# Two expert units as one from the denominator's absolute value on, and weights converted in larger steps

## The chip, the cores and the metric

The kernel runs on one core of a Trainium2 chip. A core has five engines that work through their own queues in order: PE (matmul), DVE (vector), ACT (scalar, with activation functions), POOL (elementwise work) and SP (here it only issues DMAs). The metric is the device time in microseconds (us); the time of several runs is given by its median. A profiled execution is one more run, of which a trace is kept.

## The reference

A delta-rule attention gives the rows of x, and a feed-forward layer with a rational activation follows. The shapes: 4 batches, 8 heads, 768 steps, head size 48; 3072 tokens, width 384, hidden width 2048.

```
for t in range(S):                                # S = 768, per batch and head
    y[t] = q[t] @ state
    v_old = state.T @ k_n[t]                      # k_n: keys, normalized
    state = state + beta[t] * outer(k_n[t], v[t] - v_old)
x = y, heads side by side                         # 3072 x 384
h = x @ w_in                                      # 3072 x 2048
P = a0 + a1*h + a2*h^2 + a3*h^3
Q = 1 + |b0|*|h| + |b1|*h^2
out = (P / (Q + 1e-6)) @ w_out                    # 3072 x 384
```

The two weight matrices come as 64-bit floats, the rest as 32-bit floats.

## The kernel before

The time axis is cut into 12 chunks of 64 steps (`NCH`). Within a chunk the attention is done in blocks by matmuls; 256 tokens (4 batches of 64, `TG`) leave each chunk. The hidden width is cut into 8 units of 256 columns (`NU`), so the feed-forward work is 96 units, numbered through: unit n is chunk n // 8, columns n % 8. Numbers are kept as sums of two 16-bit floats (`split16`), so a product takes three matmul passes (`PASSES`).

The weights are read once, ahead of the units. `load_in(i)` and `load_out(i)` take one unit each; `to_f32` turns 64-bit words into 32-bit floats, in pieces of 256 columns (`w_in`) and 192 columns (`w_out`): a DMA into a staging tile, an absolute value on ACT (L316), a clamp on POOL (L317), and three DVE instructions (L318, and L325 twice). The staging tiles take turns among the nine buffers of the tags mw, mu and mr (three each, `MB`). A unit's weights are scaled by a power of two found from their sums of squares, and split into two 16-bit parts; of `w_out` one half of each unit is scaled and subtracted on POOL (L243, L230), the other on DVE (L232). `tables` and `scalars` make the six coefficients per unit (`tab`, and `msc` for a chunk).

A unit's steps: `hidden(n)` makes the product ph in PSUM (18 matmuls, L808). `numerator(n)` takes its absolute value and a linear term on ACT (L826, L828), then three DVE instructions (L830, L832, L833), with an absolute value of the denominator on ACT between (L831). `quotient(n)` takes the logarithm and the exponential of minus that on ACT (L841, L842), which is the reciprocal, then three DVE instructions (L844, L845, L846; a correction of the quotient, whose middle result goes into the next unit's ph in PSUM), and a product on POOL (L847). `accumulate(n)` multiplies both 16-bit parts g by the weights (12 matmuls, L862).

One loop over n writes the program: numerator of unit n, quotient of n-1, one eighth of the attention of later chunks (`attention`), accumulate of n-2, hidden of n+1. The DVE instructions of units keep this order among themselves (`in_order`); all others are put in each engine's queue by a scheduler, from priorities and its own model of durations. ph has two PSUM buffers, each of u, w and r three SBUF buffers. The attention for the last chunks runs out before the units do, so the last units stand alone.

## Time and profile before

| | |
|---|---|
| time, median of 3 runs | 843.07 us (842.95 to 843.18) |
| profiled execution: its own time, its span | 849.25 us, 845.5 us |
| mean granted PE clock | 0.944 |
| PE, DVE, ACT, POOL busy | 74%, 88%, 73%, 40% of the span |
| DMA moved | 111.46 MB, mean 132 GB/s |

The span runs from the first to the last instruction. In a row of the profile, L844 is line 844 of the kernel, "mg<-mu,msc,mr" are the tiles written and read, "128x512" is partitions by elements, and x96 is how often; behind the bar stand the busy time in all, the mean duration in ns, and how long the engine had been idle before such instructions and for whom. All 111 MB are issued from the queues of SP and ACT.

### The profile page before, as it was taken

The page shows a single profiled execution, that of the slowest core. Times are in us where ns is not written, and L with a number is a line of the kernel's source. Part 1 is how long each engine was busy: PE and PEld are TensorE (multiplying, and loading weights), DVE is VectorE, ACT ScalarE, POOL GpSimd, SP SyncE. Part 2 cuts the span into 40 slices and gives each one's busy share as a digit, 9 for nine tenths or more (in the row PEclk, how much of TensorE's full clock was granted, in tenths as well). Part 3 has the DMA queues.
Part 4 walks back from the last instruction along what each step waited for, and adds up shares of the span by engine and source line. Part 5 has one row for each costly group of instructions (what it writes and reads, how often), then busy time and mean ns, then how long its engine had stood idle before and what let it go on. Part 6 is the DMA issues. An engine that isn't in the chain of part 4 may idle for free.

```text
span 845.5 us, 23179 instructions
## 1 busy us (share of the span) xinstructions
PE 627.7 (74%) x9264; PEld 493.8 (58%) x9264; DVE 740.2 (88%) x1405; ACT 617.1 (73%) x1278; POOL 338.1 (40%) x322
## 2 busy tenths in 40 slices
...
GB/s 237 249 212 170 225 155 170 123 140 169 157 130 165 146 120 191 146 140 183 93 145 187 71 176 150 119 193 105 98 167 111 110 103 80 76 2 21 1 19 19
DMA packets 466507, 111.46 MB, mean 132 GB/s; under 512 B 431328, under 2 KB 463072, under 8 KB 466400
## 3 DMA queue, kind: packets, MB, share of 16 engines
...
## 4 chain that ended last, share of the span: by engine, by line
DVE 34%; PE 19%; DMA 17%; SPq 11%; ACT 10%; issue 7%; POOL 1%; ACTq 0%; DVEq 0%; POOLq 0%
PE ph L808 7%; PE po L862 5%; DVE ph L845 4%; DVE w_out L325 4%; DVE mg L844 3%; DVE mw L830 3%; DVE mu L833 3%; DVE mu L832 3%; SPq L119 3%; PE pu L401 2%; DMA tq<-xdq 2%; DMA gd<-g 2%; DMA tk<-xdk 2%; SPq L475 2%; DVE mu L846 2%
## 5 line engine op out<-in xcount | busy, mean ns | idle before, releaser
L862 PE MATMUL po<-w_out,mg 128*128 128x384 f16 x1152 | 226.5, 339 | 33.3 <-DVE mg L844 20.9
L847 POOL TENSOR_TENSOR mg<-mu,mr 128x512 f16<-128x512 f32 x96 | 124.8, 1300 | 258.1 <-DVE mu L846 203.8
L808 PE MATMUL ph<-xT,w_in 128*128 128x256 f16 x1728 | 216.3, 280 | 14.1 <-DVE mu L846 11.2
L808 PEld LDWEIGHTS <-w_in 128*128 128x128 f16 x1728 | 169.8, 101 | 51.1 <-DVE mu L846 14.4
L862 PEld LDWEIGHTS <-mg 128*128 128x128 f16 x1152 | 109.5, 101 | 103.4 <-DVE mg L844 27.7
L401 PEld LDWEIGHTS <-kbd 128*128 128x128 f16 x1680 | 66.7, 109 | 47.8 <-issue 43.3
L830 DVE SCALAR_TENSOR_TENSOR mw<-mr,msc,ph 128x512 f32<-128x512 f32 x96 | 71.1, 741 | 22.1 <-ACT mu L828 21.9
L831 ACT ACTIVATE mw<-mw 128x512 f32<-128x512 f32 x96 | 60.4, 629 | 39.7 <-DVE mw L830 39.2
L845 DVE SCALAR_TENSOR_TENSOR ph<-mw,msc,mg 128x512 f32<-128x512 f32 x96 | 81.4, 848 | 1.0
L844 DVE SCALAR_TENSOR_TENSOR mg<-mu,msc,mr 128x512 f16<-128x512 f32 x96 | 81.1, 844 | 0.0
L826 ACT ACTIVATE mr<-ph,msc 128x512 f32<-128x512 f32 x96 | 65.2, 679 | 18.7 <-PE ph L808 6.9
L828 ACT ACTIVATE mu<-ph,coef,msc 128x512 f32<-128x512 f32 x96 | 74.2, 773 | 0.0
L846 DVE SCALAR_TENSOR_TENSOR mu<-mu,msc,ph 128x512 f32<-128x512 f32 x96 | 71.1, 741 | 1.4
L833 DVE SCALAR_TENSOR_TENSOR mu<-mu,msc,ph 128x512 f32<-128x512 f32 x96 | 70.7, 736 | 1.0
L841 ACT ACTIVATE mr<-mw,msc 128x512 f32<-128x512 f32 x96 | 69.2, 721 | 1.7
L401 PE MATMUL pu<-z,ebd 128*128 128x48 f16 x1728 | 54.9, 185 | 18.1 <-DVE z L232 13.5
L401 PEld LDWEIGHTS <-ebd 128*128 128x128 f16 x1728 | 53.9, 98 | 21.7 <-issue 19.4
L832 DVE TENSOR_TENSOR mu<-ph,mu 128x512 f32<-128x512 f32 x96 | 65.5, 682 | 0.0
L842 ACT ACTIVATE mr<-mr 128x512 f32<-128x512 f32 x96 | 60.3, 628 | 1.3
L401 PEld LDWEIGHTS <-wbd 128*128 128x128 f16 x1152 | 37.7, 99 | 35.9 <-issue 34.8
L230 POOL TENSOR_TENSOR mm<-m,mm 128x1024 f16<-128x1024 f32 x12 | 29.2, 2436 | 73.6 <-ACT mm L226 64.5
L401 PE MATMUL pm<-tq,kbd 128*128 128x64 f16 x576 | 27.0, 220 | 20.1 <-DMA tq<-xdq 18.3
...
## 6 DMA issues: line engine op xcount, KB each, us to landing
...
```

What stands on the lines that cost most here:

```text
L401: nc.tensor.matmul(dst[p][:, h], head(bd, lp, p * H + h), head(rt, rp, p * H + h), start=start and n == 0 and h == 0, stop=stop and n == l ...
L808: nc.tensor.matmul(ph[:, i], w_in[:, f2, wp, cc, i * P : (i + 1) * P], x[:, xp, cc], start=k == 0, stop=k == 3 * NCC - 1,)
L828: nc.scalar.activation(u, ph, AF.Identity, scale=A3, bias=a2)
L830: in_order(nc.vector.scalar_tensor_tensor(out=w, in0=z, scalar=B0, in1=ph, op0=ALU.add, op1=ALU.mult))
L832: in_order(nc.vector.tensor_mul(u, ph, u))
L833: in_order(nc.vector.scalar_tensor_tensor(out=u, in0=u, scalar=A1, in1=ph, op0=ALU.add, op1=ALU.mult))
L841: nc.scalar.activation(r, w, AF.Ln, bias=Q0)
L844: in_order(nc.vector.scalar_tensor_tensor(out=g[:, 0], in0=u, scalar=A0, in1=r, op0=ALU.add, op1=ALU.mult))
L845: in_order(nc.vector.scalar_tensor_tensor(out=t, in0=w, scalar=Q0, in1=g[:, 0], op0=ALU.add, op1=ALU.mult))
L846: in_order(nc.vector.scalar_tensor_tensor(out=u, in0=u, scalar=A0, in1=t, op0=ALU.add, op1=ALU.subtract))
L847: nc.gpsimd.tensor_mul(g[:, 1], u, r)
L862: nc.tensor.matmul(po[p], g[:, gp, i, p * P : (p + 1) * P], w_out[:, f2, wp, i], start=f2 == lo and i == 0 and k == 0, stop=f2 == hi - 1 a ...
```

## The change

Two neighbouring units, an even and an odd one, become one from the absolute value of the denominator on. `numerator` still works by units of 512 elements up to L821; at the odd unit the absolute value, logarithm and exponential follow at once, over 1024 elements (L824, L825, L826). `quotient(m)` works on pair m: three DVE instructions of 1024 elements (L837, L838, L839) and one POOL product (L840). The correction's middle result goes into w in SBUF instead of the next unit's ph. u, w and z of a pair are one tile mx with two buffers; g of a pair is one tile mg with two buffers. In the loop the quotient of pair n/2 - 1 is written at even n, behind the even unit's numerator, and accumulate comes three units later instead of two.

The weights are handled in four steps of two units (`NS`): one scale for 512 columns, words in groups of 768 per unit (two DMAs of 768 KB a step), staged in the two mx buffers; the absolute value and the clamp work in place. Both halves of `w_out` are split on ACT and DVE. `dynamic_dma_scratch_size=2048` is set where the program is built; the rest follows from the counts (`GRP = 2` steps are the same four units as before).

```diff
-    MB = 3
+    MB = 2
...
+    NS = NU // 2
...
-    def to_f32(t, src, nm, keep=MIN_NORMAL):
+    def to_f32(t, srcs, nm, keep=MIN_NORMAL):
         n = t.shape[-1]
-        st = staged([P, n, 2], U32, "ws" + nm)
-        nc.sync.dma_start(out=st.rearrange("p f w -> p (f w)"), in_=src)
-        wl, wh = st[..., 0], st[..., 1]
-        a = sb.tile([P, n], F32, tag="mg", name="wa" + nm, bufs=MB)
-        nc.scalar.activation(a, wh.bitcast(F32), AF.Abs)
-        nc.gpsimd.tensor_scalar(a, a, 3.0e38, keep, op0=ALU.min, op1=ALU.max)
-        nc.vector.tensor_scalar(
-            t, a.bitcast(U32), 3, KEEP, op0=ALU.logical_shift_left, op1=ALU.bitwise_and
-        )
...
+        st = sb.tile([P, len(srcs), n, 2], U32, tag="mx", name="ws" + nm, bufs=MB)
+        for h, src in enumerate(srcs):
+            w, x = st[:, h], t[:, h]
+            nc.sync.dma_start(out=w.rearrange("p (a f) w -> p a (f w)", a=src.shape[1]), in_=src)
+            wl, wh = w[..., 0], w[..., 1]
+            nc.scalar.activation(x.bitcast(F32), wh.bitcast(F32), AF.Abs)
+            nc.gpsimd.tensor_scalar(x.bitcast(F32), x.bitcast(F32), 3.0e38, keep, op0=ALU.min, op1=ALU.max)
+            nc.vector.tensor_scalar(x, x, 3, KEEP, op0=ALU.logical_shift_left, op1=ALU.bitwise_and)
+            for word, scalar, op0 in ((wh, 0xC0000000, ALU.bitwise_and), (wl, 29, ALU.logical_shift_right)):
+                nc.vector.scalar_tensor_tensor(out=x, in0=word, scalar=scalar, in1=x, op0=op0, op1=ALU.bitwise_or)
...
-        for j in range(2):
-            if j == 0:
-                split16((w_out[:, i, 0, j], w_out[:, i, 1, j]), to[j].bitcast(F32), ss[:, 1:2])
-            else:
-                scaled(to[j].bitcast(F32), ss[:, 1:2])
-                split16((w_out[:, i, 0, j], w_out[:, i, 1, j]), to[j].bitcast(F32), eng=nc.gpsimd)
+        for i in us:
+            split16((w_out[:, i, 0], w_out[:, i, 1]), t[:, i % 2], ss[:, 1:2])
...
     def numerator(n):
...
+        if i == 0:
+            both[m] = {"x": sb.tile([P, 3, 2, 2, TG], F32, tag="mx", name=f"mx{m}", bufs=MB)}
+        u, w, z = (both[m]["x"][:, x, i] for x in range(3))
         nc.scalar.activation(z, ph, AF.Abs, scale=B1)
         nc.scalar.activation(u, ph, AF.Identity, scale=A3, bias=a2)
         in_order(nc.vector.scalar_tensor_tensor(out=w, in0=z, scalar=B0, in1=ph, op0=ALU.add, op1=ALU.mult))
-        nc.scalar.activation(w, w, AF.Abs)
         in_order(nc.vector.tensor_mul(u, ph, u))
         in_order(nc.vector.scalar_tensor_tensor(out=u, in0=u, scalar=A1, in1=ph, op0=ALU.add, op1=ALU.mult))
+        if i == 1:
+            w, r = (both[m]["x"][:, x].rearrange("p i a t -> p (i a t)") for x in (1, 2))
+            nc.scalar.activation(w, w, AF.Abs)
+            nc.scalar.activation(r, w, AF.Ln, bias=Q0)
+            nc.scalar.activation(r, r, AF.Exp, scale=-1.0)
...
-    def quotient(n):
+    def quotient(m):
...
-        t = unit[min(n + 1, NCH * NU - 1)]["ph"]
-        nc.scalar.activation(r, w, AF.Ln, bias=Q0)
-        nc.scalar.activation(r, r, AF.Exp, scale=-1.0)
-        g = sb.tile([P, 2, 2, TG], F16, tag="mg", name=f"mg{n}", bufs=MB)
...
+        x = d.pop("x").rearrange("p x i a t -> p x (i a t)")
+        u, w, r = (x[:, i] for i in range(3))
+        g = d["g"] = sb.tile([P, 2, 2, 2, TG], F16, tag="mg", name=f"mg{m}", bufs=2)
+        g0, g1 = (g[:, i].rearrange("p i a t -> p (i a t)") for i in range(2))
+        in_order(nc.vector.scalar_tensor_tensor(out=g0, in0=u, scalar=A0, in1=r, op0=ALU.add, op1=ALU.mult))
+        in_order(nc.vector.scalar_tensor_tensor(out=w, in0=w, scalar=Q0, in1=g0, op0=ALU.add, op1=ALU.mult))
+        in_order(nc.vector.scalar_tensor_tensor(out=u, in0=u, scalar=A0, in1=w, op0=ALU.add, op1=ALU.subtract))
+        nc.gpsimd.tensor_mul(g1, u, r)
...
-    for n in range(N + 2):
+    for n in range(N + 3):
...
-        if 0 <= n - 1 < N:
-            quotient(n - 1)
+        if n % 2 == 0 and 2 <= n <= N:
+            quotient(n // 2 - 1)
         attention(*divmod(n + SHIFT, NU))
-        if 0 <= n - 2 < N:
-            accumulate(n - 2)
+        if 0 <= n - 3 < N:
+            accumulate(n - 3)
...
+    nc = _bacc.Bacc("TRN2", target_bir_lowering=False, num_devices=1, dynamic_dma_scratch_size=2048)
```

The change moves instructions. Three places show it. In the rows, ph_88 is the product of unit 88, mr88, mu88 and mw88 are its three tiles before, and mx43 and mg43 are the tiles of pair 43 (units 86 and 87) after. The first place is ACT's queue near the end, at units 88 to 90, before:

```order
L826 ACTIVATE mr89_13763<-ph_89_13744,msc_11_13589 128x512
L828 ACTIVATE mu89_13765<-ph_89_13744,coef_99,msc_11_13589 128x512
L842 ACTIVATE mr88_13716<-mr88_13716 128x512
L831 ACTIVATE mw89_13767<-mw89_13767 128x512
L841 ACTIVATE mr89_13763<-mw89_13767,msc_11_13589 128x512
L842 ACTIVATE mr89_13763<-mr89_13763 128x512
L826 ACTIVATE mr90_13815<-ph_90_13796,msc_11_13589 128x512
L828 ACTIVATE mu90_13817<-ph_90_13796,coef_99,msc_11_13589 128x512
```

and ACT's queue at units 86 to 88, after:

```order
L817 ACTIVATE mx43_12604<-ph_87_12627,msc_10_11890 128x512
L818 ACTIVATE mx43_12604<-ph_87_12627,coef_99,msc_10_11890 128x512
L748 ACTIVATE sf_11_12490<-sf_11_12490,kp_11_0_12549 128x1
L748 ACTIVATE sf_11_12490<-sf_11_12490 128x2
L824 ACTIVATE mx43_12604<-mx43_12604 128x1024
L825 ACTIVATE mx43_12604<-mx43_12604,msc_10_11890 128x1024
L817 ACTIVATE mx44_12685<-ph_88_12666,msc_11_12571 128x512
L818 ACTIVATE mx44_12685<-ph_88_12666,coef_99,msc_11_12571 128x512
L826 ACTIVATE mx43_12604<-mx43_12604 128x1024
```

What stood between a denominator and the next unit's first two instructions (L826, L828) is now L824 and L825 of double length, and L817 and L818 of the even unit stand behind them.

The second place is DVE's queue at the same units; before:

```order
L830 SCALAR_TENSOR_TENSOR mw88_13720<-mr88_13716,msc_11_13589,ph_88_13697 128x512
L832 TENSOR_TENSOR mu88_13718<-ph_88_13697,mu88_13718 128x512
L833 SCALAR_TENSOR_TENSOR mu88_13718<-mu88_13718,msc_11_13589,ph_88_13697 128x512
L844 SCALAR_TENSOR_TENSOR mg87_13727<-mu87_13671,msc_10_12856,mr87_13669 128x512
L845 SCALAR_TENSOR_TENSOR ph_88_13697<-mw87_13673,msc_10_12856,mg87_13727 128x512
L846 SCALAR_TENSOR_TENSOR mu87_13671<-mu87_13671,msc_10_12856,ph_88_13697 128x512
L830 SCALAR_TENSOR_TENSOR mw89_13767<-mr89_13763,msc_11_13589,ph_89_13744 128x512
L832 TENSOR_TENSOR mu89_13765<-ph_89_13744,mu89_13765 128x512
L833 SCALAR_TENSOR_TENSOR mu89_13765<-mu89_13765,msc_11_13589,ph_89_13744 128x512
```

and after:

```order
L819 SCALAR_TENSOR_TENSOR mx43_12604<-mx43_12604,msc_10_11890,ph_87_12627 128x512
L820 TENSOR_TENSOR mx43_12604<-ph_87_12627,mx43_12604 128x512
L821 SCALAR_TENSOR_TENSOR mx43_12604<-mx43_12604,msc_10_11890,ph_87_12627 128x512
L819 SCALAR_TENSOR_TENSOR mx44_12685<-mx44_12685,msc_11_12571,ph_88_12666 128x512
L820 TENSOR_TENSOR mx44_12685<-ph_88_12666,mx44_12685 128x512
L821 SCALAR_TENSOR_TENSOR mx44_12685<-mx44_12685,msc_11_12571,ph_88_12666 128x512
L837 SCALAR_TENSOR_TENSOR mg43_12691<-mx43_12604,msc_10_11890 128x1024
L838 SCALAR_TENSOR_TENSOR mx43_12604<-mx43_12604,msc_10_11890,mg43_12691 128x1024
L839 SCALAR_TENSOR_TENSOR mx43_12604<-mx43_12604,msc_10_11890 128x1024
L819 SCALAR_TENSOR_TENSOR mx44_12685<-mx44_12685,msc_11_12571,ph_89_12708 128x512
L820 TENSOR_TENSOR mx44_12685<-ph_89_12708,mx44_12685 128x512
L821 SCALAR_TENSOR_TENSOR mx44_12685<-mx44_12685,msc_11_12571,ph_89_12708 128x512
```

The quotient's three instructions stood behind each unit's numerator; now they stand behind the even unit's only, and the odd unit's numerator (ph_87) is followed at once by that of the next even unit (ph_88).

The third place is ACT's queue in the middle, at unit 63 and the next chunk's first. The names g, gl, kp, sh and z are attention tiles and scalars. Before:

```order
L228 ACTIVATE z_9_2_11304<-pu_9_10922,zmask_85 128x768
L516 ACTIVATE g_11_11123<-pg_11_11074 128x1024
L831 ACTIVATE mw63_11010<-mw63_11010 128x512
L761 ACTIVATE kp_8_0_10846<-kp_8_0_10846 128x1
L226 CAST gl_11_11127<-g_11_11123 128x768
L841 ACTIVATE mr63_11006<-mw63_11010,msc_7_9757 128x512
L777 ACTIVATE kp_8_0_10846<-kp_8_0_10846 128x1
L842 ACTIVATE mr63_11006<-mr63_11006 128x512
```

and after:

```order
L824 ACTIVATE mx31_10044<-mx31_10044 128x1024
L503 ACTIVATE g_11_10248<-pg_11_10199 128x1024
L825 ACTIVATE mx31_10044<-mx31_10044,msc_7_8947 128x1024
L228 ACTIVATE sh_10_10846<-S16_133,sc_10_9303 128x768
L226 CAST gl_11_10252<-g_11_10248 128x768
L826 ACTIVATE mx31_10044<-mx31_10044 128x1024
L817 ACTIVATE mx32_10286<-ph_64_10267,msc_8_10006 128x512
L818 ACTIVATE mx32_10286<-ph_64_10267,coef_99,msc_8_10006 128x512
```

The copy of g and the cast to gl now stand between the odd unit's denominator and the next even unit's two instructions, which come behind the exponential.

127 lines of the change are left out of this document (56 added, 71 removed).

## The prediction

> **What bounds the kernel now.** I read the engine table of the page first, then the busy time by stretches of the run, then the groups with their shapes kept apart, and last the timeline near the end, where the moved work stands alone. The page says that no engine is full over the whole span:
>
> ```profile
> PE 627.7 (74%) x9264; PEld 493.8 (58%) x9264; DVE 740.2 (88%) x1405; ACT 617.1 (73%) x1278; POOL 338.1 (40%) x322
> ```
>
> The stretches tell more (columns: stretch, its length, busy us of each engine, granted clock, DMA share, GB/s). I cut where the weights begin and end, where the first unit starts, and where the DVE's attention work has nearly run out:
>
> ```profile
> core 0: us, PE busy (x) PEld busy (x) DVE busy (x) ACT busy (x) POOL busy (x), PEclk, DMA share, GB/s
> 18.00:134.00 116.00, 35.64 (x582) 30.57 (x581) 111.32 (x311) 81.15 (x215) 66.32 (x90) 0.99 0.93 206
> 134.00:150.00 16.00, 11.96 (x141) 9.28 (x142) 7.51 (x27) 11.84 (x36) 6.99 (x6) 0.63 0.93 159
> 150.00:704.00 554.00, 454.22 (x7111) 360.80 (x7111) 486.58 (x863) 409.49 (x818) 214.14 (x171) 0.93 0.82 139
> 704.00:845.00 141.00, 124.85 (x1424) 92.28 (x1421) 126.09 (x197) 108.07 (x200) 37.67 (x29) 0.99 0.14 28
> ```
>
> While the weights are converted (18 to 134 us) DVE is busy 111.3 of 116 us, and the DMA engines 93%. In the main loop DVE leads with 88%, PE has 82%. At the end DVE has 89%, with no DMA to speak of. So DVE's instructions are the right thing to count, but 67 us of DVE idleness in the loop say that its order and its waits count as well. The changed groups:
>
> ```profile
> L845 DVE SCALAR_TENSOR_TENSOR ph<-mw,msc,mg 128x512 f32<-128x512 f32 x96 | 81.4, 848 | 1.0
> L844 DVE SCALAR_TENSOR_TENSOR mg<-mu,msc,mr 128x512 f16<-128x512 f32 x96 | 81.1, 844 | 0.0
> L846 DVE SCALAR_TENSOR_TENSOR mu<-mu,msc,ph 128x512 f32<-128x512 f32 x96 | 71.1, 741 | 1.4
> L232 DVE SCALAR_TENSOR_TENSOR z<-pu,zmask,z 128x768 f16<-128x768 f32 x36 | 36.3, 1007 | 2.5 <-ACT z L228 2.3
> L847 POOL TENSOR_TENSOR mg<-mu,mr 128x512 f16<-128x512 f32 x96 | 124.8, 1300 | 258.1 <-DVE mu L846 203.8 <-ACT ob L876 12.9 <-ACT kp L761 9.4
> L240 ACT ACTIVATE sq<-q 128x768 f32<-128x768 f32 x12 | 10.1, 842 | 20.6 <-DMA q<-in_q_dram 11.3 <-DMA k<-in_k_dram 5.6 <-DVE nrm L492 2.8
> ```
>
> **Term 1, fewer and longer DVE instructions.** The same kind of instruction takes 741 ns for 512 elements (L846) and 1007 for 768 (L232): 1.04 ns per element and 209 ns fixed. One of 1024 takes 741 + 512 x 1.04 = 1273 ns. L844 and L845 cost more than L846 at equal length, and the view of one line says why: the median is that of L846, a few are far longer.
>
> ```profile
> L844 DVE SCALAR_TENSOR_TENSOR mg<-mu,msc,mr x96: 731/746/1898, 159.8 to 834.9; 128x512 f16<-128x512 f32 x96
> ```
>
> The excess of the mean is 844 - 746 = 98 ns. L844 reads both tensors from SBUF; L846, which reads one from PSUM, has no such excess. After the change all three read two SBUF tensors, so I give each 0.1 us more. A pair of units costs 2 x (844 + 848 + 741) = 4866 ns before and 3 x (1273 + 100) = 4119 after: 0.75 us less. For the 36 pairs up to unit 71, which lie in the loop under attention work, that is 27 us of DVE time.
>
> [...]
>
> [...]
>
> **Term 2, the new wait at the odd unit.** The end of the run shows the unit's bare rhythm, DVE first, then ACT, then PE:
>
> ```profile
> 822.02 0.74 DVE L830 SCALAR_TENSOR_TENSOR mw<-mr,msc,ph 128x512 f32<-128x512 f32 x1
> 822.68 0.68 DVE L832 TENSOR_TENSOR mu<-ph,mu 128x512 f32<-128x512 f32 x1
> 823.40 0.75 DVE L833 SCALAR_TENSOR_TENSOR mu<-mu,msc,ph 128x512 f32<-128x512 f32 x1
> 824.07 0.74 DVE L844 SCALAR_TENSOR_TENSOR mg<-mu,msc,mr 128x512 f16<-128x512 f32 x1
> 824.85 0.76 DVE L845 SCALAR_TENSOR_TENSOR ph<-mw,msc,mg 128x512 f32<-128x512 f32 x1
> 825.64 0.75 DVE L846 SCALAR_TENSOR_TENSOR mu<-mu,msc,ph 128x512 f32<-128x512 f32 x1
> 826.31 0.74 DVE L830 SCALAR_TENSOR_TENSOR mw<-mr,msc,ph 128x512 f32<-128x512 f32 x1
> ```
>
> ```profile
> 822.80 0.63 ACT L831 ACTIVATE mw<-mw 128x512 f32<-128x512 f32 x1 [0.99 <-DVE mw L830]
> 823.46 0.72 ACT L841 ACTIVATE mr<-mw,msc 128x512 f32<-128x512 f32 x1
> 824.22 0.63 ACT L842 ACTIVATE mr<-mr 128x512 f32<-128x512 f32 x1
> 824.75 0.67 ACT L826 ACTIVATE mr<-ph,msc 128x512 f32<-128x512 f32 x1
> 825.32 0.77 ACT L828 ACTIVATE mu<-ph,coef,msc 128x512 f32<-128x512 f32 x1
> ```
>
> ```profile
> 822.16 2.14 PE L808 MATMUL ph<-xT,w_in 128*128 128x256 f16 x18
> 824.14 2.20 PE L862 MATMUL po<-w_out,mg 128*128 128x384 f16 x12
> ```
>
> DVE runs without a gap, 826.31 - 822.02 = 4.29 us per unit, 8.58 per pair. ACT has the next unit's L826 and L828 done long before, behind three short instructions. In the changed order (first place shown with the change, units 86 to 88) the odd unit's denominator is followed on ACT by an absolute value and a logarithm of 1024 elements, then by the next unit's two, and only then may DVE start that unit. ACT's slope is (842 - 629)/256 = 0.83 ns per element, with 842 from the 768-row and the 0.63 us of the 512-rows above, so 512 more elements are 0.43 us. From the start of the odd unit's first DVE instruction: 0.74 itself, 0.04 to ACT, 0.66 + 0.43 to the logarithm, 0.72 + 0.43 - 0.10 to the next independent one (0.10 is the overlap, 0.63 against 824.75 - 824.22), 0.57, 0.77, 0.02 back: 4.28 us. DVE's own work in that time is 0.66 + 0.72 + 0.67 = 2.05; it waits 2.23 us. The even unit takes 0.66 + 0.72 + 0.67 as now and then the three long steps, each 0.53 us (512 elements) above 0.78, 0.79 and 0.67: 5.88. The pair takes 10.16 us instead of 8.58. PE needs two times 2.14 + 2.20 less the overlaps, under 8.7, and does not bind. From pair 36 on the order of DVE has next to nothing to fill the gap with; for the 11 pairs 36 to 46 that is 11 x 1.58 = +17 us.
>
> In the 36 earlier pairs attention instructions stand in that gap, on both engines. The bounds are no wait at all and 2.2 us per pair, 80 us. With the groups' durations put on the changed order's rows, gap by gap, ACT outlasts DVE in about half of the gaps, by 36 us in all, an estimate. The worst kind is once per chunk, where a 1024-element copy and a 768-element cast are in ACT's way:
>
> ```profile
> L516 ACT ACTIVATE g<-pg 128x1024 f32<-128x1024 f32 x12 | 12.3, 1023 | 6.6 <-PE pg L401 5.5 <-POOL nrm L494 1.0
> L226 ACT CAST gl<-g 128x768 f16<-128x768 f32 x12 | 12.8, 1065 | 0.0
> ```
>
> Not all of it is new, for DVE waits in the same place already (columns: us in total, times, longest):
>
> ```profile
> DVE mw L830 <- ACT mu L828: 16.9, 12, 4.2
> ```
>
> That row is of the stretch 150 to 704. I take 23 us of new waiting. With term 1 the middle gains 27 - 23 = 4 us; its bounds are -27 and, with all 36, +9.
>
> **Term 3, the weights.** Their DVE rows before:
>
> ```profile
> L325 DVE SCALAR_TENSOR_TENSOR w_out<-wso,w_out 128x192 uint32<-128x192 uint32 x56 | 24.3, 449 | 0.4
> L325 DVE SCALAR_TENSOR_TENSOR w_out<-wsi,w_out 128x256 uint32<-128x256 uint32 x48 | 21.8, 469 | 0.3
> L318 DVE TENSOR_SCALAR w_out<-wai 128x256 uint32<-128x256 uint32 x24 | 10.6, 441 | 4.7 <-POOL wai L317 4.7
> L318 DVE TENSOR_SCALAR w_out<-wao 128x192 uint32<-128x192 uint32 x28 | 10.4, 373 | 0.0
> L232 DVE SCALAR_TENSOR_TENSOR w_out<-w_out,vss 128x384 f16<-128x384 f32 x7 | 5.0, 711 | 1.3 <-ACT w_out L228 0.7 <-ACT lgx L258 0.6
> ```
>
> That is 67 us without the last row, and some 5 for the 12 instructions on the last unit's own tile (4 x 0.37 + 8 x 0.45). After, 16 and 32 instructions of 768: 441 + 512 x 1.06 (the slope of 441 and 373) = 0.98, and 469 + 512 x 1.04 = 1.0 us, 48 us together: -24. Half of the split of w_out comes over from POOL, 16 halves instead of 8 (711 ns for 384, some 1.1 us for 768): +3. Four of eight small scale chains go, some 1 us each: -4. DVE loses 25 us of work here; ACT's and POOL's pieces also merge, off the path, since DVE is the full one. But it need not be 25 us of time: the DMA engines' share of 0.93 in the 116 us is 108 us of transfers, and the bytes stay, so if those bind, 8 us is all. The two staging buffers now hold whole steps, so the next load waits until both its halves are converted, where nine small buffers turned one by one; and the 16 us between weights and first unit (DVE busy 7.5) is a chain that nothing shortens. Bounds 0 and -25; I take -9, near the DMA's limit. The scratch of 2 KB costs nothing: every load and store is issued by SP or ACT.
>
> **Term 4, the end.**
>
> ```profile
> 830.59 0.74 DVE L830 SCALAR_TENSOR_TENSOR mw<-mr,msc,ph 128x512 f32<-128x512 f32 x1
> 838.25 1.26 POOL L847 TENSOR_TENSOR mg<-mu,mr 128x512 f16<-128x512 f32 x1 [1.51 <-DVE mu L846]
> 840.27 1.05 ACT L876 ACTIVATE ob<-po,kp 128x384 f32<-128x384 f32 x2 [6.86 <-PE po L862]
> ```
>
> From the last unit's first DVE instruction to the last copy: 9.7 us. After: 0.78 to ACT, 1.09 and 1.19 to the exponential, 1.09 to DVE, 1.31 + 1.32 + 1.27 there, 0.17 to POOL, a product between 1.3 and 2.6 us (say 2.3), then 16 matmuls instead of 4 at 2.20/12 = 0.18 each, 2.9: 13.4 us. **+4 us.**
>
> **The sum.** -9 (weights), -4 (middle), +17 (bare pairs), +4 (end) = +8 us. The profiled execution took 849.25 us with a span of 845.5, 6 us above the runs' median of 843.07; the difference is put on the median: **851 us**.
>
> **Rivals.** *The gap is filled (faster).* DVE is the fullest engine, and 67 us of its idleness in the loop are waits on attention that arrives late; a wait at the odd unit then only moves one that came later anyway. Then the middle gains its 27 us less some 5, the weights 15, and the bare pairs and the end still cost 21: 843 - 22 - 15 + 21 = 827 us. It decides where the new wait stays under 0.75 us per pair in the middle. For it: DVE's lead in every stretch. Against it: in-order queues, where ACT's lateness also delays the attention's casts behind it.
>
> *Two buffers are too few (slower still).* The next but one pair's first ACT instruction writes where POOL's product reads. Before, a buffer came back three units later; now POOL has from the end of the quotient to about 2.9 us after it (0.74 + 0.04 + 1.09 + 1.05), and its product takes up to 2.6, behind any attention piece in its queue. If a quarter of the 36 pairs lose 1.5 us, that is +13: 864 us. Against it: POOL is 39% busy in the loop.
>
> [...]
>
> *No change.* Gains and losses cancel to within 0.2% (1.7 us, about what this kernel's runs can tell): 843 us.
>
> **Chances.** Forecast 0.45, filled gap 0.34, buffers 0.08, port 0.05, no change 0.08. The range runs from 829, just above the filled gap's time, to 867, with both slower rivals; about one in ten lies beyond each end. The likeliest case alone has 844 to 860. Faster by over 0.2%: 0.34; within: 0.09; slower: 0.57.
>
> **What the profile after would show.** Term 1: the 1024-element groups at 1.27 to 1.4 us, 48 each, and DVE's busy time near 740 - 36 - 25 = 680 us. Term 2: a pair of 10.2 us near the end with DVE idle 2.2 us before the even unit's first instruction, put down to ACT's L818; the same row at some 40 us or more in total. Term 3: the first unit near 141 us instead of 150. I am wrong if the bare pairs run at 8.6 us or less, if the loop before them shortens by more than 20 us, or if the first unit starts before 130.

## The result and the profile after

The changed kernel takes 905.0 us (median of 4 runs, 901.5 to 907.3) against 843.0 before: a ratio of 1.074 [1.069, 1.078], 62 us slower. The direction was forecast, the size was not: 851 us, with a range up to 867. The profiled execution took 907.3 us, its span is 905.6.

The engine line of the page after, which answers to the first line of the prediction:

```profile
PE 642.7 (71%) x9264; PEld 509.4 (56%) x9264; DVE 720.6 (80%) x1113; ACT 584.2 (65%) x1046; POOL 315.6 (35%) x218
```

DVE is 20 us less busy than before, where 60 were forecast, and each engine is busy for a smaller share of a longer span: all of them wait more. To see where, I took the start of each unit's first DVE instruction (L830 before, L819 after) from the two timelines:

| us | before | after | change | forecast |
|---|---|---|---|---|
| first unit starts | 150.3 | 156.1 | +5.8 | -9 |
| from there to unit 72 ("the middle") | 568.9 | 599.6 | +30.7 | -4 |
| unit 72 to unit 94 (the last pairs) | 107.1 | 123.7 | +16.6 | +17 |
| unit 94 to the last unit, 95 | 4.3 | 5.9 | +1.6 | none |
| last unit to the end of the span | 14.9 | 20.3 | +5.4 | +4 |

The rows add up to the spans, 845.5 and 905.6 us. The last pairs and the end came as worked out; the first unit and the middle, 36 of the 60 us, had the wrong sign. The middle by stretches, before and then after (columns as in the prediction):

```profile
150.00:719.00 569.00, 468.50 (x7342) 372.26 (x7342) 499.32 (x883) 421.23 (x840) 217.96 (x174) 0.93 0.81 138
```

```profile
156.00:756.00 600.00, 475.59 (x7260) 380.32 (x7260) 498.77 (x772) 403.44 (x728) 215.49 (x132) 0.90 0.76 129
```

DVE issues 111 instructions fewer and is busy just as long (499 us); its idle time goes from 70 to 101 us. So the middle has two questions: where the 27 us of saved DVE work went, and what DVE waits for.

**The saved work.** The merged groups of the whole run after:

```profile
L839 DVE SCALAR_TENSOR_TENSOR mx<-mx,msc 128x1024 f32<-128x1024 f32 x48 | 67.6, 1409 | 0.4
L838 DVE SCALAR_TENSOR_TENSOR mx<-mx,msc,mg 128x1024 f32<-128x1024 f32 x48 | 66.4, 1384 | 0.3
L837 DVE SCALAR_TENSOR_TENSOR mg<-mx,msc 128x1024 f16<-128x1024 f32 x48 | 63.8, 1329 | 4.8 <-ACT mx L826 4.8
```

Together 4122 ns per pair; 4119 were forecast. Counted without the overlap of neighbours, all unit instructions of DVE in the middle take 280.5 us instead of 301.9. But everything else on DVE there takes 218.0 instead of 197.1: attention instructions that read two SBUF tensors got longer. Two of them in the middle, before and then after:

```profile
L566 DVE TENSOR_TENSOR pr<-ab,wt 128x512 f32<-128x512 f32 x10 | 11.3, 1126 | 0.0
...
L578 DVE SCALAR_TENSOR_TENSOR wh<-wt,wh 128x256 f16<-128x256 f32 x10 | 4.5, 455 | 0.0
```

```profile
L553 DVE TENSOR_TENSOR pr<-ab,wt 128x512 f32<-128x512 f32 x10 | 16.4, 1645 | 0.1
...
L565 DVE SCALAR_TENSOR_TENSOR wh<-wt,wh 128x256 f16<-128x256 f32 x10 | 8.6, 857 | 0.0
```

**The waits.** Rows of the waits in the middle (us in total, times, longest), by the engine that waits, before and then after; z is an attention tile that ACT and DVE write in turn from PE's product pu:

```profile
PE po L862 <- DVE mg L844: 20.2, 10, 7.0
...
PE pu L401 <- DVE z L232: 7.0, 7, 2.6
PE ph L808 <- DVE mu L846: 6.7, 9, 2.4
...
ACT z L228 <- PE pu L401: 1.6, 4, 0.8
...
DVE mw L830 <- ACT mu L828: 16.9, 12, 4.2
...
DVE z L232 <- ACT z L228: 2.3, 1, 2.3
```

```profile
PE ph L795 <- DVE mx L821: 28.5, 18, 4.8
PE px L723 <- DVE m L642: 18.2, 6, 5.6
...
PE pu L388 <- DVE z L232: 14.3, 11, 4.4
...
ACT z L228 <- PE pu L388: 27.4, 9, 9.2
...
DVE mx L819 <- ACT mx L818: 13.4, 13, 2.0
...
DVE z L232 <- ACT z L228: 10.0, 11, 2.6
```

The row in which I had put the new waiting (L819 for L818) did not grow here; another 3.9 us of L819's waits are put down to a different ACT instruction, which makes 17.3 us against 16.9. What grew is a ring: PE waits for DVE (for a product's PSUM buffer, and for z), ACT waits for PE, DVE's attention steps wait for ACT. Over all such rows, DVE's attention instructions wait 47 us for ACT instead of 18, ACT's attention instructions 51 us for PE instead of 8, PE's attention matmuls 45 us for DVE instead of 21. Some rows fell: the accumulates (po) waited 20.2 us for DVE's L844 before and for no DVE instruction after, and DVE's attention instructions wait 13 us for PE instead of 25. With these counted, PE's waits for DVE still go from 47 to 73 us, and the 29 us more that DVE's attention instructions wait for ACT come near DVE's 31 us more of idle time. The rows say who waited for whom; they do not say which wait begins the ring.

### The profile page after: what moved, and what is told of

It is laid out like the page before. It is cut to its first block, busy times and chain, and to the rows that moved or that the text cites. A ratio compares the mean times of both kernels' runs of the same rounds, so it can differ in the third digit from the quotient of the medians.

```text
span 905.6 us, 22248 instructions
## 1 busy us (share of the span) xinstructions
PE 642.7 (71%) x9264; PEld 509.4 (56%) x9264; DVE 720.6 (80%) x1113; ACT 584.2 (65%) x1046; POOL 315.6 (35%) x218
## 4 chain that ended last, share of the span: by engine, by line
DVE 33%; DMA 18%; PE 18%; ACT 11%; SPq 9%; issue 7%; POOL 3%; POOLq 0%; ACTq 0%; DVEq 0%
PE ph L795 6%; PE po L856 5%; DVE mx L838 4%; DVE mx L819 4%; DVE mg L837 4%; DVE mx L821 3%; DVE mx L820 3%; DVE mx L839 2%; DMA kbd<-tk 2%; SPq L119 2%; PE pu L388 2%; DMA tk<-xdk 2%; DMA xdk<-kn 2%; DVE pr L553 2%; DMA q<-in_q_dram 2%
## 5 line engine op out<-in xcount | busy, mean ns | idle before, releaser
L840 POOL TENSOR_TENSOR mg<-mx 128x1024 f16<-128x1024 f32 x48 | 113.6, 2367 | 243.0 <-DVE mx L839 203.0
L819 DVE SCALAR_TENSOR_TENSOR mx<-mx,msc,ph 128x512 f32<-128x512 f32 x96 | 71.1, 741 | 45.0 <-ACT mx L818 27.7
L824 ACT ACTIVATE mx<-mx 128x1024 f32<-128x1024 f32 x48 | 50.7, 1055 | 81.4 <-DVE mx L819 81.3
L817 ACT ACTIVATE mx<-ph,msc 128x512 f32<-128x512 f32 x96 | 65.2, 680 | 19.5 <-PE ph L795 17.2
L818 ACT ACTIVATE mx<-ph,coef,msc 128x512 f32<-128x512 f32 x96 | 74.3, 774 | 0.0
L821 DVE SCALAR_TENSOR_TENSOR mx<-mx,msc,ph 128x512 f32<-128x512 f32 x96 | 71.0, 739 | 1.1
L839 DVE SCALAR_TENSOR_TENSOR mx<-mx,msc 128x1024 f32<-128x1024 f32 x48 | 67.6, 1409 | 0.4
L837 DVE SCALAR_TENSOR_TENSOR mg<-mx,msc 128x1024 f16<-128x1024 f32 x48 | 63.8, 1329 | 4.8 <-ACT mx L826 4.8
L838 DVE SCALAR_TENSOR_TENSOR mx<-mx,msc,mg 128x1024 f32<-128x1024 f32 x48 | 66.4, 1384 | 0.3
L820 DVE TENSOR_TENSOR mx<-ph,mx 128x512 f32<-128x512 f32 x96 | 65.4, 681 | 0.0
L825 ACT ACTIVATE mx<-mx,msc 128x1024 f32<-128x1024 f32 x48 | 54.9, 1144 | 0.5
L826 ACT ACTIVATE mx<-mx 128x1024 f32<-128x1024 f32 x48 | 50.5, 1053 | 0.1
L230 POOL TENSOR_TENSOR mm<-m,mm 128x1024 f16<-128x1024 f32 x12 | 29.9, 2494 | 54.5 <-ACT mm L226 54.5
```

Source lines behind the costliest of these rows:

```text
L817: nc.scalar.activation(z, ph, AF.Abs, scale=B1)
L818: nc.scalar.activation(u, ph, AF.Identity, scale=A3, bias=a2)
L819: in_order(nc.vector.scalar_tensor_tensor(out=w, in0=z, scalar=B0, in1=ph, op0=ALU.add, op1=ALU.mult))
L820: in_order(nc.vector.tensor_mul(u, ph, u))
L821: in_order(nc.vector.scalar_tensor_tensor(out=u, in0=u, scalar=A1, in1=ph, op0=ALU.add, op1=ALU.mult))
L837: in_order(nc.vector.scalar_tensor_tensor(out=g0, in0=u, scalar=A0, in1=r, op0=ALU.add, op1=ALU.mult))
```

## The experiments

Sixteen kernels, each against the kernel before on the same chip. "Middle" and "bare pair" are as above (the latter the mean of the five pairs from unit 84 to 94); DVE's busy and idle time are those of the middle, from whole us to whole us.

| | run | ratio [95%] | first unit | middle | bare pair | DVE busy / idle |
|---|---|---|---|---|---|---|
| | before | 1 | 150.3 | 568.9 | 8.8 | 499 / 70 |
| | changed | 1.074 [1.069, 1.078] | 156.1 | 599.6 | 10.3 | 499 / 101 |
| 1 | weights alone | 1.015 [1.008, 1.021] | 154.0 | 574.7 | 8.9 | 493 / 81 |
| 2 | pairs alone | 1.077 [1.073, 1.081] | 148.6 | 613.5 | 10.3 | 499 / 115 |
| 3 | ACT by units | 1.047 [1.043, 1.052] | 154.0 | 585.1 | 10.0 | 490 / 96 |
| 4 | burst and quotient later | 1.120 [1.115, 1.125] | 155.2 | 634.1 | 12.0 | 502 / 132 |
| 5 | product in halves | 1.069 [1.063, 1.075] | 154.2 | 607.9 | 10.2 | 483 / 125 |
| 6 | tiles apart | 1.060 [1.052, 1.067] | 154.2 | 608.0 | 9.2 | 493 / 115 |
| 7 | no product | 1.042 [1.036, 1.048] | 154.6 | 592.2 | 9.4 | 481 / 111 |
| 8 | transfers in pieces | 1.064 [1.059, 1.070] | 154.3 | 597.9 | 10.3 | 501 / 97 |
| 9 | DVE by units | 1.121 [1.114, 1.128] | 153.9 | 640.5 | 11.6 | 520 / 121 |
| 10 | attention earlier | 1.061 [1.056, 1.066] | 154.8 | 595.8 | 10.2 | 496 / 100 |
| 11 | before, scale by 512 | 1.008 [1.005, 1.012] | 146.1 | 571.1 | 8.8 | 501 / 70 |
| 12 | before, middle result in SBUF | 1.016 [1.011, 1.021] | 150.5 | 575.1 | 8.9 | 527 / 48 |
| 13 | tiles apart, ACT by units | 1.036 [1.033, 1.039] | 152.3 | 596.4 | 9.3 | 499 / 97 |
| 14 | before, product in halves | 0.997 [0.994, 0.999] | 149.7 | 561.0 | 8.8 | 497 / 64 |
| 15 | both numerators first | 1.030 [1.025, 1.034] | 154.3 | 587.7 | 9.0 | 493 / 94 |
| 16 | before, quotients side by side | 1.028 [1.023, 1.032] | 149.5 | 581.9 | 9.6 | 515 / 67 |

### Runs 1 and 2: each half of the change alone

Run 1 keeps the changed kernel's weights and puts the unit instructions and the loop back (512 elements, on halves of the pair's tile):

```diff
-        if i == 1:
-            w, r = (both[m]["x"][:, x].rearrange("p i a t -> p (i a t)") for x in (1, 2))
-            nc.scalar.activation(w, w, AF.Abs)
+        nc.scalar.activation(w, w, AF.Abs)
...
+        t = unit[min(n + 1, NCH * NU - 1)]["ph"]
...
-        if n % 2 == 0 and 2 <= n <= N:
-            quotient(n // 2 - 1)
+        if 0 <= n - 1 < N:
+            quotient(n - 1)
```

Run 2 keeps the pairs and loads the weights by pieces, with one scale for 512 columns as in the changed kernel:

```diff
-        st = sb.tile([P, len(srcs), n, 2], U32, tag="mx", name="ws" + nm, bufs=MB)
+        tag, bufs = STAGES[stage[0] % len(STAGES)]
+        st = sb.tile([P, n, 2], U32, tag=tag, name="ws" + nm, bufs=bufs)
...
+            for e in range(2):
+                cl = slice(e * DM // 2, (e + 1) * DM // 2)
+                to_f32(to[j][:, cl], w64[f * P : (f + 1) * P, e * DM : (e + 1) * DM], f"o{f}_{e}", gate)
```

> The changed kernel's weights (steps of 1024 elements, words in groups of 768, one scale for 512 columns, scratch of 2 KB), but the units apart: every instruction of a unit as before the change, in halves of the pair's tiles. Theory P (the pairing costs the 62 us: the absolute value, logarithm and exponential of the odd unit in one burst, and the quotient, the POOL product and the accumulates in blocks): the first unit starts at 156 us as after the change, 6 later than before, the units then run as before, and the time is 849 us, 845 to 856. Theory W (the large weight steps delay the attention of the first chunks and shift the order in which the scheduler puts it beside the units, and that costs most of the 31 us in the middle): 843 + 6 + some 25 = 874 us, with units 8 to 46 late as after the change and bare units at 4.3 us.

> The paired units of the changed kernel, but the weights read in pieces of 256 and 192 columns as before, through seven small staging buffers, half of w_out split on POOL; one scale for 512 columns stays. Theory P: the first unit starts near 150 us, the middle loses its 31 us, bare pairs run at 10.2 us (+17), the end is 5 longer: 843 + 53 = 896 us, 888 to 902. Theory W: the middle is back at the predicted -4, the rest stays: 843 - 4 + 17 + 5 = 861 us.

The weights cost 1.5% (12 us), the pairs 7.7% (65 us). Theory P holds in kind, the pairing is the main cause; but run 2 lies above its range, the weights cost twice the 6 us given them, and the two sum to 77 us, not 62. Each kernel gets a new order from the scheduler, and sums of such parts hold here only to some 15 us. The spans also carry the spread of the runs: the profiled run of the kernel before took 6 us more than its median.

### Runs 3, 4 and 9: ACT's burst or the blocks

Run 3 issues the three ACT instructions by units, run 4 writes the pair's burst behind the next even unit's two and the quotient a unit later, run 9 issues the quotient, the product and the accumulates by units. From the changed kernel, in this order:

```diff
-        if n % 2 == 0 and 2 <= n <= N:
-            quotient(n // 2 - 1)
+        if 0 <= n - 1 < N:
+            reciprocal(n - 1)
+        if n % 2 == 0 and 2 <= n <= N:
+            quotient(n // 2 - 1)
```

```diff
-        if n % 2 == 0 and 2 <= n <= N:
-            quotient(n // 2 - 1)
+        if n % 2 == 0 and 2 <= n <= N:
+            reciprocal(n // 2 - 1)
+        if n % 2 == 1 and 3 <= n <= N + 1:
+            quotient((n - 3) // 2)
```

```diff
-        if n % 2 == 0 and 2 <= n <= N:
-            quotient(n // 2 - 1)
+        if 2 <= n < N + 2:
+            quotient(n - 2)
```

`reciprocal` holds the absolute value (in run 4), the logarithm and the exponential, of a unit in run 3 and of a pair in run 4. In run 4 the accumulates also come one unit later.

> The changed kernel, with the denominator's absolute value, the logarithm and the exponential by units of 512 at the places they had before; the quotient, the POOL product and the accumulates stay by pairs. Theory P1 (of the pairing it is ACT's burst at the odd unit that costs): DVE no longer waits for L818 in the bare pairs, which take 2 x 2.1 + 3 x 1.32 = 8.2 us instead of 10.2, the middle gains back some 30: 905 - 22 - 30 = 853 us, 845 to 862. Theory P2 (it is the blocks of DVE, POOL and PE: quotient of 4 us at a stretch, 24 matmuls at a stretch): the bare pairs gain their 20, the middle stays: 885 us. Theory W: 880 to 885 as well, and the first run of this call tells it from P2.

> The changed kernel, with the absolute value, logarithm and exponential of a pair kept whole (1024 elements) but written behind the next even unit's two ACT instructions, and the quotient one unit later. Theory P1: ACT's burst of 3.3 us then lies beside the even and the odd unit's six DVE instructions (4.2 us), the wait of DVE for L818 goes from 27.7 us in the middle and 2.2 us in each bare pair to near nothing: 905 - 22 - 25 + 3 (a unit's longer drain at the end) = 861 us, 850 to 872. Theory P2 or W: the bare pairs alone gain: 886 us. Where two buffers for the pair's tile are too few, the first ACT instructions of a pair wait for the product of the pair before the last, which now ends one unit later: over 890 us.

> The changed kernel with the other half undone: ACT keeps its burst of 1024 elements at the odd unit, but the quotient's three DVE instructions, POOL's product and the accumulates go by units of 512 again, the even unit's at the next even unit, the odd unit's one unit later. With units apart on all engines (856 us), apart on ACT alone (885) and apart on none (905) this closes the square. Theory burst (the attention's DVE steps wait for attention instructions of ACT, 47 us in the middle against 18 before, because those stand behind ACT's burst): the time stays at 890 us or more. Theory blocks (the quotient's 3.9 us at a stretch, the 2.4-us product and 24 matmuls at a stretch delay the attention's chain): 862 to 880 us, and in the bare pairs DVE always has a quotient between two units, so that they come to 8.6 to 9.2 us.

Without the burst the kernel gains 2.6% or 22 us (ratios 1.074 and 1.047), 15 of them in the middle; so it is worth a third of the loss. The 885.0 us are theory P2's number by luck: P2 had the gain in the bare pairs, and these stay at 10.0, where theory P1 said 8.2. The third run's rows show why; ACT, POOL and DVE around one even unit, the first three ACT rows being of the odd unit before it:

```profile
846.71 0.63 ACT L822 ACTIVATE mx<-mx 128x512 f32<-128x512 f32 x1 [2.37 <-DVE mx L819]
847.38 0.72 ACT L829 ACTIVATE mx<-mx,msc 128x512 f32<-128x512 f32 x1
848.13 0.63 ACT L830 ACTIVATE mx<-mx 128x512 f32<-128x512 f32 x1
848.66 0.67 ACT L817 ACTIVATE mx<-ph,msc 128x512 f32<-128x512 f32 x1
849.23 0.77 ACT L818 ACTIVATE mx<-ph,coef,msc 128x512 f32<-128x512 f32 x1
```

```profile
846.19 2.36 POOL L843 TENSOR_TENSOR mg<-mx 128x1024 f16<-128x1024 f32 x1 [7.68 <-DVE mx L842]
```

```profile
845.94 0.74 DVE L819 SCALAR_TENSOR_TENSOR mx<-mx,msc,ph 128x512 f32<-128x512 f32 x1
...
850.09 0.75 DVE L819 SCALAR_TENSOR_TENSOR mx<-mx,msc,ph 128x512 f32<-128x512 f32 x1 [2.03 <-ACT mx L818]
```

From the odd unit's first DVE instruction to the end of the even unit's second ACT instruction it takes 850.00 - 845.94 = 4.06 us, five short ACT instructions in a row. The same five took 826.09 - 822.02 = 4.07 us in the kernel before, and 4.26 in the changed kernel with its burst (864.84 to 869.10). So the burst lengthens this chain by 0.2 us only. What changed is the DVE work beside it: six instructions of 4.29 us before, three of 2.05 once the quotient stands behind the even unit alone. Theory P1's 8.2 left that chain out.

The rival of the two buffers is in the same place: L817 writes into the tile that POOL's product reads until 846.19 + 2.36 = 848.55. But ACT is not idle before L817, and L817 follows L830 by 0.53 us as the next instruction did in the kernel before (824.22 to 824.75), so this row can't tell the two apart. In runs 4 and 9 the product ends a unit later. Run 4 went where its last expectation put this rival, over 890 (945.7 us); run 9 took 950.0 us. In both, ACT's L817 waits for the product, 62.3 and 32.7 us. Run 9 was meant to tell burst from blocks and, with that wait in it, doesn't.

### Runs 5, 7 and 14: POOL's product

Run 5 cuts the changed kernel's product in two, run 14 does it in the kernel before (256 elements each), run 7 fills the second 16-bit part with zeros instead:

```diff
-        nc.gpsimd.tensor_mul(g1, u, r)
+        for h in range(2):
+            s = slice(h * 2 * TG, (h + 1) * 2 * TG)
+            nc.gpsimd.tensor_mul(g1[:, s], u[:, s], r[:, s])
```

```diff
-        nc.gpsimd.tensor_mul(g1, u, r)
+        nc.gpsimd.memset(g[:, 1].bitcast(F32), 0.0)
```

> The changed kernel, with POOL's product of a pair in two instructions of 512 elements. In the middle the changed kernel's DVE was busy as long as before (498.8 us in the stretch from the first unit to unit 72, against 499.3), though its unit instructions had fallen by 26 us: attention instructions of DVE that read two SBUF tensors had got longer by 19 us (the 512-element product of attention 1645 ns instead of 1126, the 256-element one 857 instead of 455). Theory port (those instructions wait for the 2.4-us POOL product to end, where it was 1.3 us): with halves of 1.3 us they come back by half or more, DVE's busy time in the middle falls to 480 to 490 us, and the time to some 893 us, 885 to 900. Theory order (they vary with what happens to stand beside them, and the waits set the time): DVE's busy time stays within 5 us and the time is 900 to 910 us.

> The changed kernel, with POOL's product replaced by a fill with zeros of the same tile (the second 16-bit part of the quotient is left out). POOL then reads nothing for it. Theory port: DVE's attention instructions fall back below their durations of before, the three quotient instructions to the 1.28 us that they have in the bare pairs, DVE's busy time in the middle falls by 25 to 35 us, and the time to 870 to 885 us. Theory order: under 10 us. The two-buffer theory: the pair's tile comes free 2.4 us sooner, so the bare pairs shorten (ACT's first instruction of a pair no longer meets the product's end) to 9.5 us or less; if ACT's burst alone bound them they stay at 10.2 us.

> The kernel before, with POOL's product of a unit in two instructions of 256 elements. In the changed kernel halves of the product took 17 us off DVE's busy time and nothing off the run. Here DVE is 88% busy, and one line that made it 28 us busier cost 14 us. Theory port bounds (a DVE instruction that reads two SBUF tensors waits for the POOL instruction under way, so shorter ones make it wait less): L844 and L845 fall from 845 ns towards 790, DVE is busy 10 to 20 us less, and the time is 833 to 840 us. Theory waits (what DVE no longer does it waits): busy time falls as much, and the time stays at 841 to 847 us.

The middle of run 5:

```profile
154.00:762.00 608.00, 481.41 (x7355) 383.90 (x7355) 482.52 (x771) 401.95 (x728) 220.25 (x167) 0.90 0.75 128
```

With halves DVE is 16 us less busy there, as theory port said, and the run is not shorter: what DVE no longer does it waits. This is the plainest evidence against the first step of my sum, by which less DVE work is less time. Without the product, run 7 gains 27 us, 12 of them between units 72 and 94. Its DVE and ACT near the end:

```profile
849.33 0.75 DVE L821 SCALAR_TENSOR_TENSOR mx<-mx,msc,ph 128x512 f32<-128x512 f32 x1
849.99 0.74 DVE L819 SCALAR_TENSOR_TENSOR mx<-mx,msc,ph 128x512 f32<-128x512 f32 x1
...
852.83 1.28 DVE L837 SCALAR_TENSOR_TENSOR mg<-mx,msc 128x1024 f16<-128x1024 f32 x1 [0.71 <-ACT mx L826]
```

```profile
848.15 0.69 ACT L817 ACTIVATE mx<-ph,msc 128x512 f32<-128x512 f32 x1 [4.15 <-DVE mx L839]
848.74 0.77 ACT L818 ACTIVATE mx<-ph,coef,msc 128x512 f32<-128x512 f32 x1
849.40 1.05 ACT L824 ACTIVATE mx<-mx 128x1024 f32<-128x1024 f32 x1
```

The even unit follows the odd one without a gap, and ACT's burst is all there, but behind the even unit's two instructions: the tile is free when the quotient ends, and they stand ahead of the burst in this order. DVE now waits 0.7 us at the quotient instead. So what made the 2.2 us is the place of the two instructions in ACT's queue; that the scheduler put them there because the tile is free sooner is likely, not shown. The time is in theory port's range (870 to 885), but DVE's busy time in the middle fell by 18 us, not by 25 to 35, and over the run the quotient's three came to 1361, 1504 and 1443 ns, no shorter than after the change. What they meet is POOL's other work: of the 18 that took over 1380 ns in the changed kernel, all stand beside attention instructions of POOL, each ending 1.06 to 1.09 us after the end of one, and none beside the product. In the kernel before, halves (run 14) take only 3 us off DVE (740.2 to 737.2), not the 10 to 20 of theory port, and the time is in theory waits' range; the ratio of 0.997 [0.994, 0.999] just leaves out no change. It is the one version here that beats both kernels.

### Run 12: the middle result in SBUF, and nothing else

```diff
-        t = unit[min(n + 1, NCH * NU - 1)]["ph"]
+        t = w
```

> The kernel before with one line of the change: the correction's middle result goes to w in SBUF instead of the next unit's product in PSUM. Theory port (the two later instructions of the quotient now read two tensors in SBUF, and meet POOL's product and the attention's): DVE is busy 10 us more, and the time is 848 to 856 us. Theory release (the product's PSUM buffer comes free 2.2 us sooner, and PE, which waits for it 11 us in the middle, starts the next one sooner): 834 to 842 us. Neither: 842 to 847 us.

One line costs 1.6% (13 us) and ends at 858.4, just above theory port's range and far from theory release's 834 to 842. The same instruction L846, before and then in run 12 (shortest, median, longest ns):

```profile
L846 DVE SCALAR_TENSOR_TENSOR mu<-mu,msc,ph x96: 654/747/753, 162.2 to 837.3; 128x512 f32<-128x512 f32 x96
```

```profile
L846 DVE SCALAR_TENSOR_TENSOR mu<-mu,msc,mw x96: 657/752/2864, 162.2 to 844.1; 128x512 f32<-128x512 f32 x96
```

The medians are alike, the longest is 2864 ns instead of 753. The seven L846 of over 2 us each end 0.54 to 0.55 us after the end of an attention instruction of POOL (L230), as an instruction would that waited for that end. In the trace of before the same is seen of the two that read both tensors from SBUF: of the 192 L844 and L845, 17 took over 0.95 us, and each ends 0.54 to 0.57 us after the end of a POOL instruction beside it, 14 times L230 and 3 times the product. The price was above the 0.1 us that I took: DVE is busy 28.6 us more (768.8 for 740.2), 0.3 us per unit, of which L846's own mean is 0.18 (923 ns for 741); in the changed kernel the three instructions of a pair came as forecast all the same. Part of it came back as idle time, which fell from 70 to 48 us in the middle. I had expected that from the product's PSUM buffer, which is free sooner, but PE's wait for that buffer rose, from 6.7 to 14.1 us.

### Runs 6, 13, 15 and 16: order, buffers, length

Run 6 starts from run 2: u, w, r and z have tiles of their own, the last quotient step frees u, and `linear` (a unit's two first ACT instructions) is written ahead of the burst:

```diff
-        in_order(nc.vector.scalar_tensor_tensor(out=u, in0=u, scalar=A0, in1=w, op0=ALU.add, op1=ALU.subtract))
-        nc.gpsimd.tensor_mul(g1, u, r)
+        in_order(nc.vector.scalar_tensor_tensor(out=w, in0=u, scalar=A0, in1=w, op0=ALU.add, op1=ALU.subtract))
+        nc.gpsimd.tensor_mul(g1, w, r)
...
+            linear(n)
+        if n % 2 == 0 and 2 <= n <= N:
+            reciprocal(n // 2 - 1)
+        if n < N:
             numerator(n)
```

Run 13 issues `reciprocal` by units there; run 15 then puts the quotient behind both numerators and the accumulates a unit later, with u in three buffers, z in one, and the last quotient step writing u again:

```diff
-        if n % 2 == 0 and 2 <= n <= N:
-            quotient(n // 2 - 1)
+        if n % 2 == 1 and 3 <= n <= N + 1:
+            quotient((n - 3) // 2)
```

Run 16 starts from run 12, with four buffers and the accumulates a unit later:

```diff
-        if 0 <= n - 1 < N:
-            quotient(n - 1)
+        if 0 <= n - 1 < N:
+            reciprocal(n - 1)
+        if n % 2 == 0 and 2 <= n <= N:
+            quotient(n - 2)
+            quotient(n - 1)
```

> Paired units with the weights by pieces, as in the second experiment (908.9 us), but the pair's tiles apart (u, w, r, and z of its own, two buffers each), the last quotient step writes over w so that u comes free at its end, and each unit's two first ACT instructions are written ahead of the pair's burst, the burst ahead of the next even unit's DVE work. Theory gap (between the odd unit's and the next even unit's DVE instructions stands nothing that covers ACT's chain, and the tile of the pair before the last is still being read by POOL): both are loosened, the bare pairs take 8.2 to 9.2 us instead of 10.2, and the same gap in the middle closes by a like amount: 909 - 11 - 25 = 873 us, 862 to 882. Theory blocks (quotient, product and accumulates in long blocks delay the attention's chain in the in-order queues): only the bare pairs gain: 895 us, 888 to 902.

> The sixth experiment's kernel (898 us: pairs on DVE, POOL and PE, tiles apart, the two first ACT instructions of a unit ahead, weights by pieces), with the absolute value, logarithm and exponential by units of 512. Nothing in it runs in pairs but the quotient, the product and the accumulates. Theory gap and burst (what the pairing loses are DVE's waits for ACT, whose burst also holds up ACT's half of the attention's splits): the bare pairs take 2 x 2.1 + 3.84 = 8.2 us, the middle from the first unit to unit 72 at most 575 us (569 before, 600 in the changed kernel, 608 in the sixth), the time 843 to 858 us. Theory blocks (quotient and product at a stretch, with the port, hold up the attention): bare pairs 8.2 to 8.6 us, but the middle at 585 us or more as with ACT alone by units (585), the time 862 to 878 us.

> The kernel of the thirteenth run (878 us: quotient, product and accumulates by pairs, everything else by units, tiles apart), with the pair's two numerators one behind the other and the quotient of the pair before behind both, u in three buffers. There the even unit's product in PSUM had come free before the quotient's 3.9 us and the odd one's only behind it, and PE, which works in order, waited for it 35 us in the middle (7 in the kernel before), with the attention's matmuls behind. Now both are free before the quotient begins. Theory PSUM (that wait starts the chain: PE late, ACT's half of the attention's splits late, DVE's half waits): PE waits for a product's buffer under 15 us, the middle takes at most 580 us (596 there, 569 before), the time is 848 to 862 us. Theory block (the attention's DVE step itself stands behind 3.9 us of quotient, and PE waits for that): PE's waits for the attention's DVE steps stay at 40 us or more (21 before), the middle at 590 us or more, the time 868 to 885 us.

> The kernel of the twelfth run (858 us: the kernel before with the middle result in SBUF), with the quotients of two units side by side behind the even unit's numerator, as in the changed kernel, and four buffers instead of three; every instruction keeps its 512 elements, so there is no long instruction, no ACT burst and no 2.4-us product, and the weights are as before. Theory order (it is the place of the quotients, a stretch of DVE work of the same 4.5 us, that holds up PE and the attention): the middle goes from 575 us to 590 or more, PE's waits for a product's buffer from 15 us to 25 or more, the time to 872 us or more. Theory length (the long instructions and products do it): the middle stays at 570 to 580 us and the time at 853 to 864 us.

Runs 6 and 13 loosen the bare pairs (9.2 and 9.3 us in the mean; the shortest of run 13 takes 8.5) but not the middle: 608 and 596 us. Both times (898.2 and 877.9) are in the range of theory blocks. Run 13 has no burst and no shared tile, and still PE waits at least as long for a product's buffer as in the changed kernel (28.5 us):

```profile
PE ph L820 <- DVE mu L862: 34.6, 19, 6.7
```

Run 15 puts both numerators ahead of the quotient:

```profile
PE ph L820 <- DVE mu L862: 16.9, 13, 2.1
...
PE pu L413 <- DVE z L232: 12.3, 8, 5.2
```

That wait halves, the middle gains 9 us and stays 19 above before, and the time (874.6) is in the range of theory block; PE's waits for attention steps of DVE remain at 38 us. So the late PSUM buffer is a part, not the start of it all. Run 16 has 512-element instructions throughout; against run 12 it is the place of the quotients that changed, with the buffers that this takes:

```profile
150.00:732.00 582.00, 472.44 (x7408) 377.88 (x7409) 515.15 (x882) 426.57 (x841) 239.82 (x173) 0.91 0.77 137
```

It costs 1.2% more than run 12, 10 us: 7 in the middle, and some in the bare pairs (9.6 instead of 8.9). The time (872.6) is at theory order's bound, the middle (582) between the two expectations; but PE's wait for a buffer did not grow (7.0 us), against theory order. ACT waited for POOL's product instead (26 us in the middle). So the place costs something without any long instruction, but by a wait for buffers, and this run can't part the two.

### Runs 8, 10 and 11: the weights, and the attention's place

Run 8 cuts the weight transfers, run 10 writes the attention a unit earlier (both from the changed kernel), run 11 is the kernel before with the sums of two units ahead of one scale (`sw`, `tab` and `msc` by `NS = NU // 2`):

```diff
-            nc.sync.dma_start(out=w.rearrange("p (a f) w -> p a (f w)", a=src.shape[1]), in_=src)
+            for a in range(src.shape[1]):
+                nc.sync.dma_start(out=w.rearrange("p (a f) w -> p a (f w)", a=src.shape[1])[:, a], in_=src[:, a])
```

```diff
-    SHIFT = 2
+    SHIFT = 3
```

```diff
+        if i % 2 == 0:
+            return
...
+        for x, tt in ((i - 1, halves.pop(s)[0]), (i, t)):
+            split16((w_in[:, x, 0], w_in[:, x, 1]), tt, sw[:, 0, s : s + 1])
```

> The changed kernel, with each weight transfer of 768 KB cut into pieces of 256 KB (w_in) and 384 KB (w_out); conversion, scales and buffers as in the changed kernel. Theory queue (the first units start 6 us later than before because the attention's small transfers stand behind 768-KB ones): the first unit starts at 150 us or before, and the time is 895 to 900 us. Theory buffers or order (the two staging tiles that come free as a whole, or the order of the work ahead of the first unit, hold it up): the first unit stays at 154 to 157 us and the time at 901 to 908.

> The changed kernel with the attention written one unit earlier beside the units (three units ahead instead of two). Theory late chain (with pairs, each step of the attention takes longer, and its results come late for units that are otherwise ready): the middle gets back 15 us or more, 880 to 892 us, though the first unit then starts a few us later. Theory queues (the steps wait for each other in the in-order queues whatever their place in the program): within 8 us of the changed kernel, 897 to 913 us.

> The kernel before with one scale for 512 columns, and nothing else of the change: pieces of 256 and 192 columns, nine staging buffers, POOL's half of w_out, units apart. The first experiment (all of the weights' change, units apart) took 12 us more than the kernel before. Theory steps (the large transfers, the two staging tiles that come free as a whole and the conversions in groups of 768 cost that): this one is at 839 to 846 us, with the first unit between 146 and 151 us. Theory scale (a unit's split now waits for the sums of its neighbour, so the chain ahead of the first unit gets longer): 850 to 858 us, with the first unit at 153 us or later.

Smaller transfers leave the first unit at 154.3, against theory queue, though the kernel gains about 1% (1.064 for 1.074), spread over all stretches. Written a unit earlier, the attention gives some 10 us in all (ratio 1.061 for 1.074) and 4 in the middle; the time, 897.3 us, is in the range of theory queues. One scale for 512 columns puts the first unit at 146 us, as theory steps said, yet the kernel is 0.8% slower, with theory scale's time (853.0); but for one of 863 us its ten runs spread from 847 to 857, and the profiled one was the fastest, so its rows do not show the loss. What the first unit waits for in the changed kernel, where DVE's work ahead of it did shrink, stays open:

```profile
18.00:134.00 116.00, 35.55 (x582) 30.93 (x581) 98.64 (x176) 74.11 (x137) 49.20 (x38) 0.59 0.97 215
```

The traces show one thing of it. Followed back from the first unit's first DVE instruction, from each piece to what released it, the chain holds 47 us of weight work on DVE and 24 us of the attention's transfers before, 23 and 51 us after. So the weight work on this chain did get shorter, and the attention's transfers took its place. With smaller weight transfers (run 8) it holds 33 and 25 us, and the first unit still starts at 154.3; why is not shown.

## Why the prediction failed, step by step

What the profile after was to show: the long groups at 1.27 to 1.4 us (yes, 1.33 to 1.41), DVE busy near 680 us (720.6), bare pairs of 10.2 us (yes), the even unit's wait put down to L818 with 40 us or more in all (27.7 us), the first unit near 141 us (156). In the bare pairs the view puts that wait down to PE's ph. That can't be: at 869.18 DVE starts unit 92, whose product was ready at 863.49 (counted by 18 matmuls a unit), and the product that ends at 869.16 is unit 93's. ACT's L818 of unit 92 ends at 869.10, 0.08 us before DVE's start, so the wait is L818's as forecast:

```profile
869.18 0.75 DVE L819 SCALAR_TENSOR_TENSOR mx<-mx,msc,ph 128x512 f32<-128x512 f32 x1 [2.22 <-PE ph L795]
```

```profile
868.33 0.77 ACT L818 ACTIVATE mx<-ph,coef,msc 128x512 f32<-128x512 f32 x1
```

```profile
861.36 2.13 PE L795 MATMUL ph<-xT,w_in 128*128 128x256 f16 x18
...
867.02 2.14 PE L795 MATMUL ph<-xT,w_in 128*128 128x256 f16 x18 [2.23 <-DVE mx L821]
```

None of the three signs of being wrong came: all three were of a kernel faster than the forecast.

**Term 1** was right in its rows and wrong as time. The pair's three instructions came at 4122 ns (4119 forecast) and the unit work of the middle fell by 21 us (27). The means count the overlap of neighbours as work: from the quotient's start to the next instruction behind it the bare pairs show 2 x 2.24 us before (824.07 to 826.31) and 3.84 after (861.00 to 864.84), 0.64 us less per pair instead of 0.75, which makes 23 us for 36 pairs. Above all, the sum took from the rows of the units alone. The attention's instructions gave 21 us back, so DVE was as busy as before; and run 5, where DVE was 16 us less busy and the time the same, shows that DVE's busy time no longer set the pace.

**Term 2, the middle, is the step that failed**: "With term 1 the middle gains 27 - 23 = 4 us", with +9 as the upper bound; it came at +31. It took DVE's saved work for saved time, and it put the new wait at one place, the even unit's L819, whose waits for ACT in the middle did not grow (16.9 to 17.3 us). By the wait rows the waits came where PE stands between: PE waits longer for DVE, ACT's half of the attention's splits for PE, and DVE's half for ACT. That DVE's quotient at a stretch starts it is argued from the order and borne out in part (run 15, 9 us of the middle; run 16, 7, with a wait for buffers in it), not shown for the whole. The bound +9 was a bound for that one place, not for the ring.

**Term 2, the bare pairs**, came as forecast (10.2 us, +16.6), and by the chain that I gave (4.28 us forecast, 4.34 measured from the odd unit's start at 864.84 to the even one's at 869.18). A second chain is nearly as long. The logarithm there ends at 867.85, the product's read of the tile at 867.45, and L817 starts between them, 0.10 us before the logarithm's end:

```profile
866.70 1.15 ACT L825 ACTIVATE mx<-mx,msc 128x1024 f32<-128x1024 f32 x1
867.75 0.67 ACT L817 ACTIVATE mx<-ph,msc 128x512 f32<-128x512 f32 x1
```

```profile
865.09 2.36 POOL L840 TENSOR_TENSOR mg<-mx 128x1024 f16<-128x1024 f32 x1 [7.87 <-DVE mx L839]
```

Without the burst (run 3) both chains are within 0.2 us of where they were, and the pairs take 10.0 us; without the product (run 7) ACT's order is another, and pairs of 8.7 us appear.

**Term 3** had the wrong sign. Its rows were right: the conversion instructions of DVE take 46.2 us instead of 70.6. But in the 116 us DVE's busy time fell by 13 us only (98.6 for 111.3), the attention's transfers took the place of the saved work in the chain ahead of the first unit, and that unit came 5.8 us later; with the units apart (run 1) the weights cost 12 us. Smaller transfers do not mend it (run 8). **Term 4** came near: +5.4 for +4.

The rivals *two buffers* (13 us) and *port* (in the chances and in the upper end of the range, at a size that was my estimate and that no run shows) stood as alternatives. They are no alternatives: the SBUF result alone costs 13 us (run 12), the side-by-side place, with its waits for buffers, 10 more (16 against 12), the weights 12 (run 1), the burst 22 (changed against run 3). That is 57 of the 62 us, which leaves nothing of the gain from the merging. The sum is a reading, since the parts were not added one on another in one chain of runs, and run 2 shows what such sums are worth here.

What stays open: whether the rest of the ring in the middle (run 15 is still 19 us above before) comes from the length of DVE's blocks or from how the scheduler places the attention around them, and what delays the first unit.
